# Turning normalised token rows between token order and feature order: 16 small VectorE transpositions per pair replaced by one transposition and 16 block transfers

## The chip, the cores and the metric

The kernel runs on one core of a Trainium2 chip. The metric is the device time of one execution in microseconds (us). A core has five engines that run side by side, each with its own instruction queue taken strictly in order: TensorE (PE in the profile; its weight loads are PEld), VectorE (DVE), ScalarE (ACT), GpSimd (POOL) and SyncE (SP, which here only issues DMAs). An instruction waits on semaphores until what it needs is there, and everything behind it on the same engine waits too. The 16 DMA engines are shared by all queues.

## The reference, cut to what matters

Inputs are q, k, v of shape (8, 8, 576, 64), a factor `g_ln` of 512, and two weights of 512x2048 and 2048x512, given as float64.

```python
# attention inside chunks of 64 tokens, 8 heads of 64
scores = (q_c @ k_c.T) / 8;  attn = softmax(scores);  x = attn @ v_c     # x: (8, 576, 512)
# feed-forward with a layer norm in front
xn = (x - mean(x)) / sqrt(var(x) + 1e-6) * g_ln
out = x + maximum(xn @ w_ch1, 0) @ w_ch2
```

There are 4608 tokens. The contraction of `xn @ w_ch1` runs over features, so TensorE needs `xn` with features on the 128 partitions, while attention leaves `x` with tokens on the partitions. Between the two, every block of `xn` has to be transposed. That turning is what the change is about.

## The kernel before, in words

The work is cut into 18 **pairs** of 256 tokens (two tiles of 128, index `j`), numbered 0 to 17. `attention(pair, ...)` is a Python generator that does one pair: it loads q, k, v, computes the scores (L298), the row maxima `top` (L305), the subtraction (L330) and the exponentials (L333, ScalarE), transposes the probabilities into `pt_sb` (16 VectorE transpositions of 32x256, L358, or TensorE where `by_pe` is set), sums and inverts the denominators `den` (L365 to L367), multiplies with v (L387, called PV below), scales into `x` (L421), takes mean and variance (L431, L432), `rstd` (L437, a power on GpSimd) and writes `x` to HBM for later (`spill`, L254). Then the normalised rows `xg` are made: (x - mean) * g on VectorE (L443), times `rstd` on ScalarE (L449), and turned.

Pairs 0 to 5 (tiles 0 to 2) go through an ordinary feed-forward (`ffn`, L527 and L551). The other twelve, pairs 6 to 17, are the ones with `rows_of` set. They are collected in four-pair groups of 1024 tokens: their turned rows go into two shared tiles `rows`, and `combine(half)` (L731, L734) forms from these rows sums and differences for a feed-forward that needs 7 products of half-size blocks in place of 8 (`unit_ffn`). Three such **units** follow one another. While unit u runs its products, the attention of the four pairs of unit u+1 is woven between them; the last unit has nothing beside it.

Of the twelve, pairs 6, 8 and 9 are turned on TensorE (`by_pe`, L459). The other nine, pair 7 and the eight pairs woven into the first two units, are turned on VectorE: 16 transpositions of 32 partitions x 256 elements (L467), which also put each 32x32 block into its final partition quarter.

The order of all instructions is written out by hand. Up to the units, strings (`START`, `SECOND`, `THIRD`) say which generator moves on by one `yield` between two pieces of the feed-forward. Inside a unit, `weave` counts matmuls of 128x512: a unit has 336 in the first part (the products, L778, 14 per quarter q of 6 matmuls each) and 384 in the second (L863, 192 for each half of the tokens, in steps of 4). Pair n (0 to 3) of the next unit starts at matmul `n * PAIR_SPAN + LOADED`, and its steps follow at the offsets in `STEPS`. `combine(0)` starts at 345 and `combine(1)` at 592. An offset is thus a place in the program order; what an engine does at it still waits for its data.

In the first part of a unit, the sums of a quarter sit in four PSUM banks, `c` and `a` for e = 0 and 1. ScalarE copies a bank to a snapshot (L784) and VectorE adds a snapshot to a bank, giving `hu` (L787), before the bank is used again. In the second part ScalarE makes `hh` (or `hx`), the rectified high part of `hu` (L800), and VectorE the low part `hl` (or `hx`) of it (L805), three blocks ahead of the matmuls that use them. The weights of a unit are streamed through a ring of six places of 512 KB; `ring.fetch` (L687) issues the next load on SP once the matmuls have left a place, and each place serves 12 matmuls.

Four tiles per pair (`p_sb`, `pt_sb`, `xg`, and after the change `turned`) rotate through the two buffers of the pool `work`.

## Time and profile before

| | before |
|---|---|
| median of 3 runs | 845.57 us (845.19 to 845.84) |
| profiled execution | 846.09 us, span 844.3 us |
| PE busy | 831.7 us, 99% of the span |
| DVE busy | 561.4 us, 66% |
| ACT busy | 270.8 us, 32% |
| POOL busy | 151.5 us, 18% |
| bytes moved by DMA | 192.60 MB, mean 228 GB/s |

The profiled execution is one of its own: its span runs from the first to the last recorded instruction, and its time also holds what lies around the span. In the rows below, L467 is line 467 of the kernel before, "DVE hu L787" is the VectorE instruction of line 787 that writes `hu`, and a group row gives the busy time in us, the mean of one instruction in ns, and after the bar the idle time of the engine just before them. Ends of matmuls are modelled, so a busy TensorE says little by itself; distances between starts of matmuls say more.

### The profile page before, as it was taken

How to read it: one execution, taken by the hardware profiler on the slowest of the kernel's cores; microseconds unless marked ns; L12 is line 12 of the kernel's file. 1: busy time of each engine (PE TensorE's matmuls, PEld its weight loads, DVE VectorE, ACT ScalarE, POOL GpSimd, SP SyncE). 2: the span in 40 equal slices, each digit the busy share in tenths (PEclk: the TensorE clock that was granted, in tenths of full speed). 3: DMA queues.
4: the chain of work that ended last, by engine and by line, in shares of the span. 5: the costliest groups of instructions: out<-in, count | busy, mean ns of one | idle time of the engine just before them, and what ended most of it. 6: DMA issues, size and time to landing. Idle time of an engine off the chain costs nothing.

```text
span 844.3 us, 14613 instructions
## 1 busy us (share of the span) xinstructions
PE 831.7 (99%) x5850; PEld 682.0 (81%) x5850; DVE 561.4 (66%) x957; ACT 270.8 (32%) x425; POOL 151.5 (18%) x138
## 2 busy tenths in 40 slices
PE   7999999999999999999999999999999999999998
PEld 4888888888888888888787888887878888888886
DVE  6989966787556736797999927879999421232321
ACT  5766431122322333222341402324223212232220
POOL 0111006473751223000130400001302300000000
PEclk9999999999999999999999999999999999999999
DMA  9997417938982147776786868877658776667572
GB/s 363 328 274 221 157 43 239 345 142 286 324 270 79 42 175 259 230 257 200 254 312 208 291 190 296 276 217 254 236 192 276 243 248 188 192 195 246 189 281 106
DMA packets 69043, 192.60 MB, mean 228 GB/s; under 512 B 6640, under 2 KB 20976, under 8 KB 67056
## 3 DMA queue, kind: packets, MB, share of 16 engines
q1 hardware_dynamic: 67680, 186.95, 64.1%
q0 software_dynamic: 1296, 4.72, 2.9%
q8 instruction: 46, 0.75, 0.3%
q14 instruction: 21, 0.17, 0.1%
HBM read 147.08 MB, written 39.85 MB: 221 GB/s over the span
## 4 chain that ended last, share of the span: by engine, by line
PE 84%; DVE 11%; DMA 2%; issue 1%; ACT 1%; SPq 0%; POOL 0%; ACTq 0%; DVEq 0%; POOLq 0%
PE y L778 24%; PE y L863 17%; PE y L551 15%; PE h L527 15%; PE h L863 8%; DVE pt_sb L358 3%; DVE rows L467 2%; PE s L298 2%; DMA wp<-wfs 1%; PE h L387 1%; DVE hx L805 1%; DVE top L305 1%; DMA k_t<-qkv 1%; PE s L387 1%; DVE hu L787 1%
## 5 line engine op out<-in xcount | busy, mean ns | idle before, releaser
L778 PE MATMUL y<-xc,ring 128*128 128x512 f32 x1008 | 232.5, 391 | 0.4 <-DVE hu L787 0.4
L778 PEld LDWEIGHTS y<-xc,ring 128*128 128x128 f32 x1008 | 188.3, 188 | 40.6 <-DVE hu L787 1.2
L527 PE MATMUL h<-xth,wp 128*128 128x512 f32 (+1 forms) x432 | 129.6, 370 | 1.1 <-DMA wp<-wfs 1.1
L863 PE MATMUL y<-ring,hx 128*128 128x512 f32 x486 | 128.0, 391 | 0.0
L863 PEld LDWEIGHTS y<-ring,hx 128*128 128x128 f32 x486 | 90.8, 188 | 19.0
L787 DVE TENSOR_TENSOR hu<-y,snap 128x512 f32<-128x512 f32 x72 | 49.2, 690 | 82.8 <-ACT snap L784 43.2
L551 PE MATMUL y<-wp,hh 128*128 128x512 f32 x376 | 96.2, 394 | 0.0
L527 PEld LDWEIGHTS h<-xth,wp 128*128 128x128 f32 x432 | 78.2, 188 | 15.9 <-DMA wp<-wfs 1.3
L784 ACT COPY snap<-y 128x512 f32<-128x512 f32 x72 | 42.2, 586 | 121.2 <-PE y L778 121.2
L731 POOL TENSOR_TENSOR xc<-rows,xc 128x512 fp32r<-128x512 f32 x42 | 58.7, 1413 | 123.8 <-ACT xc L730 119.8
L551 PEld LDWEIGHTS y<-wp,hh 128*128 128x128 f32 x376 | 69.1, 188 | 13.9
L358 DVE STREAM_TRANSPOSE pt_sb<-p_sb 32x256 f32<-32x256 f32 x176 | 76.7, 436 | 3.5 <-ACT p_sb L333 0.5
L527 PE MATMUL h<-xtl,wp 128*128 128x512 f32 (+1 forms) x216 | 78.3, 367 | 0.0
L541 DVE SCALAR_TENSOR_TENSOR hl<-h,hh 128x512 fp32r<-128x512 f32 (+1 forms) x53 | 33.0, 629 | 64.9 <-ACT hh L540 64.7
L863 PE MATMUL y<-ring,hh 128*128 128x512 f32 x252 | 68.9, 389 | 0.0
L467 DVE STREAM_TRANSPOSE rows<-xg 32x256 f32<-32x256 f32 x144 | 62.7, 436 | 5.4 <-ACT xg L449 3.2
L540 ACT ACTIVATE hh<-h 128x512 fp32r<-128x512 f32 (+1 forms) x53 | 28.5, 546 | 117.7 <-PE h L527 117.7
L805 DVE SCALAR_TENSOR_TENSOR hx<-hu,hx 128x512 fp32r<-128x512 f32 x54 | 43.9, 817 | 30.2 <-PE y L863 12.2
L863 PEld LDWEIGHTS y<-ring,hh 128*128 128x128 f32 x252 | 47.3, 188 | 9.9
L551 PE MATMUL y<-wp,hl 128*128 128x512 f32 x188 | 51.8, 390 | 0.0
L437 POOL TENSOR_TENSOR rstd<-vare,mhalf 128x2 f32<-128x2 f32 x12 | 10.6, 886 | 229.5 <-DVE vare L436 229.5
L863 PE MATMUL h<-ring,hx 128*128 128x512 f32 x162 | 49.9, 389 | 0.0
(130 smaller groups left out, 986.6 us busy)
## 6 DMA issues: line engine op xcount, KB each, us to landing
ring<-w2d SPq DMA_DIRECT2D x96, 512.0 KB, 4.3
ring<-wa SPq DMA_DIRECT2D x84, 512.0 KB, 4.3
raw<-w SPq DMA_DIRECT2D x15, 1024.0 KB, 7.3
out<-x SPq DMA_DIRECT2D x36, 256.0 KB, 4.5
q_t<-qkv SPq DMA_DIRECT2D x17, 512.0 KB, 5.8
k_t<-qkv SPq DMA_DIRECT2D x17, 512.0 KB, 6.8
v_t<-qkv SPq DMA_DIRECT2D x32, 256.0 KB, 6.8
w2d<-wp SPq DMA_DIRECT2D x16, 512.0 KB, 7.1
```

The source lines that it names most:

```text
L358: nc.vector.transpose(out=pt_sb[quad(2 * h2 + j), :, c, quad(i)], in_=p_sb[quad(2 * c + i), :, h2, quad(j)])
L467: nc.vector.transpose(out=to[quad(j), :, quad(i)], in_=of[quad(i), :, quad(j)])
L527: nc.tensor.matmul(h, lhsT=(wh, wh, wl)[m][:, ks], rhs=(xth, xtl, xth)[m][:, k, :], start=i == 0, stop=i == len(terms) - 1,)
L540: nc.scalar.activation(hh, h, AF.Relu)
L541: nc.vector.scalar_tensor_tensor(out=hl, in0=h, scalar=0.0, in1=hh.bitcast(F32), op0=ALU.max, op1=ALU.subtract)
L551: nc.tensor.matmul(sums(pairs[j // 2])[j % 2], lhsT=(hh, hh, hl)[m], rhs=(wh, wl, wh)[m], start=f == 0 and m == 0, stop=f == NF - 1 and m ...
L731: nc.gpsimd.tensor_tensor(out=o[:, 1], in0=x, in1=o[:, 0].bitcast(F32), op=ALU.subtract)
L778: nc.tensor.matmul(bank, lhsT=w[:, (0, 0, 1)[m], ks], rhs=x[:, (0, 1, 0)[m], k, :], start=start and k == m == 0, stop=k == 1 and m == 2, s ...
L784: nc.scalar.copy(out, bank)
L787: nc.vector.tensor_tensor(out=out, in0=bank, in1=s, op=ALU.add)
L805: nc.vector.scalar_tensor_tensor(out=hl, in0=x, scalar=0.0, in1=hh.bitcast(F32), op0=ALU.max, op1=ALU.subtract)
L863: nc.tensor.matmul(ys[j], lhsT=(hh, hh, hl)[m], rhs=w[:, (0, 1, 0)[m]], start=f == 0 and m == 0, stop=f == NF - 1 and m == 2,)
```

## The change

For the twelve pairs with `rows_of`, the centring and scaling now run on ScalarE in one instruction per tile: `Identity` with scale `rstd` and bias `-mean * rstd` (`centre`, a VectorE instruction on 128x2). The factor g is no longer applied there. It is applied after the turning, where a feature is a partition and g is one number per partition (`g_cols`, four columns that are now loaded behind `g_sb`).

For the nine pairs turned by VectorE, one transposition over 128 partitions x 1024 elements now turns every 32x32 block where it stands, into a new tile `turned`. Sixteen DMAs on SP's queue (one per pair of partition quarters: 32 partitions x 1 KB read, in two pieces of 512 B written) then carry the blocks to their places in `rows`, four to a step. Last, four ScalarE instructions over 128x256 multiply the rows by g in place. For the three pairs turned by TensorE, g goes into the evacuation of PSUM: eight ScalarE instructions of 128x128 in place of two of 128x512.

The order of tokens inside `rows` differs (by quarter `i`, then `k`), and `combine` reads it accordingly. The written-out order is changed too: `PAIR_SPAN` from 140 to 130, 19 steps in place of 18 and closer together, one step fewer for the three TensorE pairs, and some letters of `SECOND` and `THIRD` moved. A spacer tile shrinks from 176 to 144 columns.

```diff
 THIRD = {
-    0: "CS", 1: "CS", 2: "DDGS", 3: "DS", 4: "DDS", 5: "DS", 6: "DGS", 7: "GGHS", 8: "DG", 9: "D", 10: "GGP",
-    11: "HGGP", 12: "G", 13: "G", 14: "GGHP", 15: "GHP", 16: "GHP", 17: "GP", 18: "HHGP", 19: "HGP", 20: "HGP",
-    21: "HHP", 22: "HP", 24: "H", 25: "H", 26: "QQ", 27: "QR", 28: "Q", 29: "QXXN", 30: "QQR", 31: "Q",
+    0: "CS", 1: "CS", 2: "DDGS", 3: "DS", 4: "DDS", 5: "DS", 6: "GS", 7: "GGHS", 8: "DG", 9: "D", 10: "GGP",
+    11: "GGH", 12: "G", 13: "G", 14: "GGHP", 15: "GP", 16: "GHP", 17: "GGHP", 18: "GGHHP", 19: "HP", 20: "HHP",
+    21: "HP", 22: "GPP", 23: "H", 24: "H", 26: "QQ", 27: "QR", 28: "Q", 29: "QXXN", 30: "QQR", 31: "Q",
 }
-PAIR_SPAN = 140
+PAIR_SPAN = 130
 LOADED = 8
-STEPS = (0, 6, 11, 18, 26, 37, 48, 59, 68, 76, 88, 95, 102, 110, 118, 129, 140, 158)
+STEPS = (0, 6, 11, 16, 22, 30, 38, 46, 54, 60, 66, 72, 82, 88, 96, 106, 116, 126, 150)
...
-    g_sb = const.tile([P, DM], F32, name="g_sb")
+    g_all = const.tile([P, DM + NK], F32, name="g_sb")
+    g_sb, g_cols = g_all[:, :DM], g_all[:, DM:]
...
         xg = work.tile([P, 2, DM], F32, name="xg", tag="work")
-        for j in range(2):
+        if rows_of:
+            if not by_pe:
+                turned = work.tile([P, 4, 2 * NK, 32], F32, name="turned", tag="work")
+            centre = small.tile([P, 2], F32, name="centre")
             nc.vector.scalar_tensor_tensor(
-                out=xg[:, j, :], in0=x[:, j, :], scalar=mv[:, j, 0:1], in1=g_sb, op0=ALU.subtract, op1=ALU.mult
+                out=centre, in0=mv[:, :, 0], scalar=-1.0, in1=rstd, op0=ALU.mult, op1=ALU.mult
             )
-        yield
+            for j in range(2):
+                nc.scalar.activation(
+                    xg[:, j, :], x[:, j, :], AF.Identity, scale=rstd[:, j : j + 1], bias=centre[:, j : j + 1]
+                )
...
+        if rows_of and by_pe:
+            rows_t = rows_of().rearrange("p j i (k t) -> p j k i t", k=NK)
...
+                for k in range(NK):
+                    nc.scalar.activation(
+                        rows_t[:, j, k], xt[j][:, k * P : (k + 1) * P].rearrange("p (i t) -> p i t", i=4), AF.Copy,
+                        scale=g_cols[:, k : k + 1],
+                    )
+                yield
+            return
+
         if rows_of:
-            for j in range(2):
-                nc.scalar.activation(xg[:, j, :], xg[:, j, :], AF.Copy, scale=rstd[:, j : j + 1])
-            yield
...
+            nc.vector.transpose(
+                out=turned.rearrange("p b a t -> p a b t"),
+                in_=xg.rearrange("p j (k b f) -> p (j k) b f", k=NK, b=4),
+            )
+            yield
             rows_t = rows_of()
...
-                to = rows_t.rearrange("p j k t -> p (j k) t")
-                of = xg.rearrange("p j (k t) -> p (j k) t", k=NK)
-                for j in range(4):
-                    for i in range(4):
-                        nc.vector.transpose(out=to[quad(j), :, quad(i)], in_=of[quad(i), :, quad(j)])
-                    yield
+            for i in range(4):
+                for b in range(4):
+                    nc.sync.dma_start(
+                        rows_t[quad(b), :, i], turned[quad(i), b].rearrange("p (j k) t -> p j (k t)", j=2)
+                    )
+                yield
+            for k in range(NK):
+                x = rows_t.rearrange("p j i (k t) -> p (j i) k t", k=NK)[:, :, k]
+                nc.scalar.activation(x, x, AF.Copy, scale=g_cols[:, k : k + 1])
+            yield
             return
...
-        a, b = (r[:, half].rearrange("p j k t -> p k j t") for r in shared["rows"])
+        a, b = (r[:, half].rearrange("p j i (k t) -> p k (j i) t", k=NK) for r in shared["rows"])
```

More of the change, by code (lines that the diff above doesn't have):

```diff
@@ L108, in chunk_attention_ffn @@
     gap = ctx.enter_context(tc.tile_pool(name="gap", bufs=1))
-    gap.tile([P, 176], F32, name="gap")
+    gap.tile([P, 144], F32, name="gap")
     raws = ctx.enter_context(tc.tile_pool(name="raws", bufs=1))
@@ L316, in attention @@
         if pair == 0:
-            nc.sync.dma_start(g_sb, g)
+            nc.sync.dma_start(g_all, g)
         yield
@@ L445, in attention @@
             )
-        yield
+            for j in range(2):
+                nc.scalar.activation(
+                    xg[:, j, :], x[:, j, :], AF.Identity, scale=rstd[:, j : j + 1], bias=centre[:, j : j + 1]
+                )
+        else:
+            for j in range(2):
+                nc.vector.scalar_tensor_tensor(
+                    out=xg[:, j, :], in0=x[:, j, :], scalar=mv[:, j, 0:1], in1=g_sb, op0=ALU.subtract, op1=ALU.mult
+                )
+        yield
+        if rows_of and by_pe:
+            rows_t = rows_of().rearrange("p j i (k t) -> p j k i t", k=NK)
+            xt = halves()
+            for j in range(2):
+                for k in range(NK):
+                    ks = slice(k * P, (k + 1) * P)
+                    nc.tensor.transpose(out=xt[j][:, ks], in_=xg[:, j, ks], identity=ident)
+                for k in range(NK):
[5 more added lines that the diff above has]
+            return
@@ L447, in attention @@
         if rows_of:
-            for j in range(2):
-                nc.scalar.activation(xg[:, j, :], xg[:, j, :], AF.Copy, scale=rstd[:, j : j + 1])
+            nc.vector.transpose(
+                out=turned.rearrange("p b a t -> p a b t"),
+                in_=xg.rearrange("p j (k b f) -> p (j k) b f", k=NK, b=4),
+            )
             yield
-        if rows_of:
             rows_t = rows_of()
-            if by_pe:
-                xt = halves()
-                for j in range(2):
-                    for k in range(NK):
-                        ks = slice(k * P, (k + 1) * P)
-                        nc.tensor.transpose(out=xt[j][:, ks], in_=xg[:, j, ks], identity=ident)
-                    nc.scalar.copy(rows_t[:, j], xt[j].rearrange("p (k t) -> p k t", k=NK))
-                    yield
-            else:
-                to = rows_t.rearrange("p j k t -> p (j k) t")
-                of = xg.rearrange("p j (k t) -> p (j k) t", k=NK)
-                for j in range(4):
-                    for i in range(4):
-                        nc.vector.transpose(out=to[quad(j), :, quad(i)], in_=of[quad(i), :, quad(j)])
-                    yield
+            for i in range(4):
+                for b in range(4):
+                    nc.sync.dma_start(
+                        rows_t[quad(b), :, i], turned[quad(i), b].rearrange("p (j k) t -> p j (k t)", j=2)
+                    )
+                yield
@@ L469, in attention @@
+            for k in range(NK):
+                x = rows_t.rearrange("p j i (k t) -> p (j i) k t", k=NK)[:, :, k]
+                nc.scalar.activation(x, x, AF.Copy, scale=g_cols[:, k : k + 1])
+            yield
             return
@@ L1016 @@
         n: np.ascontiguousarray(a)
-        for n, a in (("qkv", qkv), ("v01", v01), ("g", np.broadcast_to(moe_g_ln, (P, DM))), ("w", w))
+        for n, a in (("qkv", qkv), ("v01", v01), ("g", g), ("w", w))
     }
```

10 lines of the change are left out of this document (6 added, 4 removed).

## The prediction

> **What bounds the kernel now.** I read the page's head first, then busy time by stage, then the chain of waits, and last the order of time around the places where TensorE stands.
>
> ```profile
> span 844.3 us, 14613 instructions
> ...
> PE 831.7 (99%) x5850; PEld 682.0 (81%) x5850; DVE 561.4 (66%) x957; ACT 270.8 (32%) x425; POOL 151.5 (18%) x138
> ```
>
> The view by stretches has, after each stretch, its length and the busy time of PE, PEld, DVE, ACT and POOL; I show the first unit and the last.
>
> ```profile
> core 0: us, PE busy (x) PEld busy (x) DVE busy (x) ACT busy (x) POOL busy (x), PEclk, DMA share, GB/s
> ...
> 326.50:502.00 175.50, 174.82 (x1235) 142.83 (x1234) 142.17 (x258) 53.73 (x91) 25.19 (x19) 1.00 0.72 243
> ...
> 677.40:844.30 166.90, 163.18 (x720) 134.77 (x719) 44.25 (x65) 38.49 (x64) 0.00 (x0) 0.99 0.63 208
> ```
>
> VectorE is busy 81% of the first unit (142.17 of 175.50), where four pairs of attention run beside the products, and 27% of the last, where none does. All pairs but one that the one transposition touches lie in the first two units. How much TensorE loses there follows from the chain of waits (start, length, what):
>
> ```profile
> 326.52 2.72 PE y L778 x12
> 329.24 1.09 PE s L298 x64
> 330.33 16.55 PE y L778 x72
> ...
> 501.88 2.72 PE y L778 x12
> ...
> 677.38 76.16 PE y L778 x336
> 753.54 43.52 PE y L863 x192
> ```
>
> In the last unit 336 products take 76.16 us, 0.2267 us each, and 192 of the second part 43.52 us, the same: its 720 matmuls take 163.2 us, with no wait. A block of scores costs 1.09 us, and the 72 products behind it 16.55 where 72 x 0.2267 is 16.32, so 1.32 us with the change of shape. Eight such blocks (four scores, four PV, taken as equal) make 163.2 + 10.6 = 173.8 us for a unit that never waits. The first took 501.88 - 326.52 = 175.36, the second 677.38 - 501.88 = 175.50. So each loses 1.6 to 1.7 us, **3.3 us together, and that is all that a lighter VectorE can win in the units**. Between the start-up and the units the chain is PE throughout. TensorE's own timeline shows where the first unit loses it:
>
> ```profile
> 403.68 4.24 PE L778 MATMUL y<-xc,ring 128*128 128x512 f32 x18
> 408.11 1.66 PE L778 MATMUL y<-xc,ring 128*128 128x512 f32 x6 [0.19 <-DVE hu L787]
> ...
> 416.07 1.16 PE L387 MATMUL h<-v_t,pt_sb 64*64 64x64 f32 x64
> ...
> 450.44 1.57 PE L387 MATMUL h<-v_t,pt_sb 64*64 64x64 f32 x64
> ...
> 452.74 0.62 PE L863 MATMUL y<-ring,hh 128*128 128x512 f32 x2
> 453.76 0.50 PE L863 MATMUL y<-ring,hl 128*128 128x512 f32 x1 [0.40 <-DVE hl L805]
> ```
>
> Eighteen products from 403.68 end at 407.76, the next starts at 408.11: 0.35. The PV block takes 1.57 where a free one takes 1.16: 0.41. Two matmuls from 452.74 end at 453.19, the next starts at 453.76: 0.57. That is 1.33; the rest of the 1.6 is scattered. All three wait for VectorE, which is behind, with the transpositions of rows among what it does:
>
> ```profile
> 395.80 3.59 DVE L467 STREAM_TRANSPOSE rows<-xg 32x256 f32<-32x256 f32 x8
> 399.42 1.23 DVE L305 TENSOR_REDUCE top<-s 128x16 f32<-128x1024 f32 x1
> 400.68 1.22 DVE L330 TENSOR_TENSOR p_sb<-s,top 128x1024 f32<-128x1024 f32 x1
> 401.93 1.80 DVE L467 STREAM_TRANSPOSE rows<-xg 32x256 f32<-32x256 f32 x4
> ```
>
> **The change, part by part.** The durations come from these groups (busy, mean of one in ns, idle before):
>
> ```profile
> L467 DVE STREAM_TRANSPOSE rows<-xg 32x256 f32<-32x256 f32 x144 | 62.7, 436 | 5.4 <-ACT xg L449 3.2
> L443 DVE SCALAR_TENSOR_TENSOR xg<-x,mv,g_sb 128x512 f32<-128x512 f32 x36 | 26.0, 762 | 0.0
> L330 DVE TENSOR_TENSOR p_sb<-s,top 128x1024 f32<-128x1024 f32 x16 | 19.5, 1219 | 0.4
> L449 ACT ACTIVATE xg<-xg,rstd 128x512 f32<-128x512 f32 x24 | 16.0, 716 | 49.8 <-DVE xg L443 25.9 <-POOL rstd L437 23.7
> L540 ACT ACTIVATE hh<-h 128x256 fp32r<-128x256 f32 x12 | 4.1, 373 | 0.8 <-PE h L527 0.8
> ```
>
> *Removed from VectorE*, per pair: 16 x 0.436 = 6.98 us of transpositions and 2 x 0.762 = 1.52 of centring. *Added*: one transposition of 128x1024, which no row shows. Its floor is the 1.22 us of another instruction of 128x1024; its ceiling is 6.98, if the four partition quarters went one after the other. I take 1.22, since 256 elements take 0.436 and 1024 of them, at the slope of other VectorE work, no more than that row. [...] `centre` is 256 values, between 0 and 0.76; I take 0.2. Net 7.1 us less per pair, 28 of the 142 in a unit.
>
> *ScalarE* does two Identity instructions in place of two Copies, at 0.716 as before, and four of 128x256 for g, between 0.373 (from PSUM) and 0.716: 0.42 each, 1.7 us per pair. Cover: ScalarE is idle for 122 us of a unit. [...] For the three pairs turned on TensorE, eight small evacuations replace two; they lie in the stage that waits for nothing, where the chain is PE.
>
> *SP and DMA*. 16 transfers per pair, none of 32 KB in the trace; the nearest:
>
> ```profile
> q1 hardware_dynamic: 67680, 186.95, 64.1%
> ...
> ring<-wa SPq DMA_DIRECT2D x84, 512.0 KB, 4.3
> ...
> v_t<-qkv SPq DMA_DIRECT2D x32, 256.0 KB, 6.8
> ...
> x_d<-x SPq DMA_DIRECT2D x14, 512.0 KB, 3.0
> ```
>
> Issue takes SP 0.42 us each (the row below), 6.7 us per pair, four in every 10 matmuls (2.27 us). SP otherwise waits for ring places, so it has the time. Behind a waiting transfer stand the ring's loads: one place of six serves 12 matmuls (2.72 us), so a load is due 13.6 us after its place is left and takes 4.3; SP may be 9 us late before TensorE notices, and it is late by 2 or 3 (the transposition) plus 1.7 (four issues). Engine time: 512 KB per pair in packets of 512 B. By bytes they are 0.3% of queue 1's 186.95 MB, 1.5 us; by packets (1024 of them at the queue's mean, 0.641 x 844.3 x 16 / 67680 = 0.128 us, over 16 engines) 8.2 us. A pair's 32 us at a share of 0.72 leaves 9. Landing lies between 3.0 and 6.8 us; I take 3.5, since the writer's side is like that of `x_d` and a ring load stands ahead. Then the last four, issued by 1.7 us after matmul 126, have landed at 5.2, and the factor step at 150 comes 24 x 0.2267 = 5.4 after it: no wait.
>
> ```profile
> 364.70 0.42 SPq L270 DMA_DIRECT2D k_t<-qkv  x1
> ```
>
> *The order.* This decides. The pair's steps are closer together: from scores to PV are 60 matmuls in place of 76. I walk the queue of VectorE for pair n = 2, whose PV now falls at matmul 330 (268 + 60, rounded up to a product), close to the change from first to second part. Durations are those of pair n = 0 in the trace, which ran without a queue:
>
> ```profile
> 330.51 1.22 DVE L305 TENSOR_REDUCE top<-s 128x16 f32<-128x1024 f32 x1
> 331.75 1.22 DVE L330 TENSOR_TENSOR p_sb<-s,top 128x1024 f32<-128x1024 f32 x1
> ...
> 334.90 3.57 DVE L358 STREAM_TRANSPOSE pt_sb<-p_sb 32x256 f32<-32x256 f32 x8 [0.27 <-ACT p_sb L333]
> ...
> 342.73 1.29 DVE L787 TENSOR_TENSOR hu<-y,snap 128x512 f32<-128x512 f32 x2
> ...
> 346.51 1.21 DVE L365 TENSOR_REDUCE den<-p_sb 128x16 f32<-128x1024 f32 x1
> ```
> ```profile
> 333.81 1.06 ACT L333 ACTIVATE p_sb<-p_sb 128x1024 f32<-128x1024 f32 x1
> ```
>
> Scores start at 0; `top` starts at 1.27 (330.51 against 329.24) and ends at 2.5; a sum `hu` waits 0.7 for its snapshot and ends at 3.9; the subtraction ends at 5.1, the exponentials at 6.2. Then 16 transpositions at 0.45 (7.2), two `hu` (1.3) and one `hl` (0.6) ahead of the last four: done at 15.3. PV is due at 1.09 + 60 x 0.2267 = 14.7, its second half, which needs the last group, 0.5 later: **0.3 late**. Behind that VectorE has one `hu` (0.6), `den` (1.6 with its two small ones), and the `hu` that frees a bank which the second matmul of the second part writes: 18.2, against 15.0 + 1.09 + 1.36 + 0.23 = 17.7: **0.5 late**. So 0.8 where 0.35 is lost today. For pair n = 3 the same walk has less in it (1.27, `top`, one `hl`, subtraction and exponentials, one L734 at 0.7, 16 transpositions, two `hl`): 14.6 against 14.7, which I count as 0.2. Pairs 0 and 1 come out about 1 us early. The third wait, at the change of halves, goes: pair 3's attention is over at matmul 524 but for its factor step, where today its transpositions run from 546 to 586. What is scattered today I keep at 0.
>
> Sum: 1.6 lost per unit today, 1.0 after, 0.6 won twice, **1.2 us**. The profiled execution took 846.09 us, its span 844.3: it becomes 843.1 in the span and 844.9 with the 1.8 around it. The median, 845.57, is 0.5 below that execution, so I forecast **844.4 us**. Own range, by 0.5 us of error in each of the two walks per unit: 842.4 to 846.4.
>
> **Rivals.**
> *All waits go.* If VectorE runs ahead a little more than in my walk (1 us in 15), nothing is left to wait for: 845.57 - 3.3 = 842.3. For it: 28 us less work per unit. Against: the compressed steps.
> *The transfers land late, and it is slower.* Place: the factor step on ScalarE, which stands ahead of the snapshots (L784), and the next pair's `pt_sb`, which takes the buffer of `turned`. It decides from a landing of 5.3 us on: the next pair's step 22 is 26 matmuls and a score block (7.0 us) behind the last group, whose issue takes 1.7. At 6.8, as for `v_t`, VectorE is 1.5 us late in three pairs per unit, less the 0.9 that pair 1 has to spare: 1.5 + 1.5 + 0.6 = 3.6, and ScalarE is 3.1 late with 2.1 to spare (two products, less 0.59) for the pairs of the first part, 1.0 twice, partly the same time. About 4.5 per unit, 9 less the 1.2: 853. For it: rows of 6.8 are in this queue. Against: those are loads from HBM, and writes from on-chip memory (`x_d`) land in 3.0.
> *The single transposition is as long as the sixteen.* Then VectorE is relieved of 1.3 us per pair alone while PV comes 16 matmuls, 3.6 us, sooner; in the second part a pair is 5.8 us heavier than in my walk, which today's 18.3 us from scores to PV swallow and 14.7 do not: 0.7 late in each of eight pairs, 845.57 + 5.6 = 851.
> *Nothing moves.* The old waits are replaced by new ones of the same size: within 1 us of before. It lies inside the forecast's own range.
>
> **How the numbers follow.** Forecast 0.47, all waits gone 0.30, late landing 0.13, long transposition 0.05, something else slower 0.05. A measurement of this kernel tells 0.2% (1.7 us) from no change. Faster by that: the 0.30 and 0.06 of the forecast's lower edge, 0.36. Slower: 0.13 + 0.05 + 0.05 less 0.03 of mild cases, 0.20. Same: 0.44. The floor of the range is the full gain, 842.2. The top reaches into the late landings and leaves out their far end: 848.2.
>
> **What would show it.** Right: DVE busy in 326 to 502 near 114 us; the transposition a row near 1.2 us; transfers landing under 5.3 us; no PE row waiting for `hl` L805 behind the change of halves; a PV at the end of a unit's first part still over 1.16 us. Wrong: a ScalarE row that waits for a DMA into `rows`, a VectorE `pt_sb` that waits for a DMA, a ring load that TensorE waits for, or a unit longer than 175.4 us.

## The result, and where the time went

| | before | after |
|---|---|---|
| median | 845.38 us (844.84 to 845.84, 4 runs) | 852.87 us (852.68 to 853.39, 4 runs) |
| ratio, 95% interval | | 1.009 (1.0072 to 1.0107) |
| span of the profiled execution | 844.3 us | 851.1 us |

The kernel became slower, by 7.5 us. The forecast was 844.4 with a top of 848.2; the rival "the transfers land late" had named 853.

The page's head of the kernel after:

```profile
span 851.1 us, 14767 instructions
...
PE 833.6 (98%) x5850; PEld 682.8 (80%) x5850; DVE 498.1 (59%) x810; ACT 290.0 (34%) x479; POOL 149.4 (18%) x138
```

VectorE got its relief, 63 us of busy time. TensorE has the same 5850 matmuls; what grew is its waiting. The chain of waits of the kernel after (start, length, what) says where:

```profile
327.49 2.72 PE y L803 x12
...
506.09 2.72 PE y L803 x12
...
683.65 76.16 PE y L803 x336
```

The first unit lasts 506.09 - 327.49 = 178.60 us (175.36 before), the second 177.56 (175.50 before), the rest up to the end of the span 167.45 (166.9 before), and the units begin 1.0 us later. So the 6.8 us are 1.0 ahead of the units, 3.2 and 2.1 in them and 0.5 in the last one. TensorE's timeline in the first unit:

```profile
376.26 0.34 PE L389 MATMUL h<-v_t,pt_sb 64*64 64x64 f32 x6
377.09 1.14 PE L389 MATMUL h<-v_t,pt_sb 64*64 64x64 f32 x58 [0.49 <-DVE pt_sb L360]
378.16 16.64 PE L803 MATMUL y<-xc,ring 128*128 128x512 f32 x72
394.73 1.16 PE L300 MATMUL s<-k_t,q_t 64*64 64x64 f32 x64
...
409.65 0.34 PE L389 MATMUL h<-v_t,pt_sb 64*64 64x64 f32 x6
410.38 1.14 PE L389 MATMUL h<-v_t,pt_sb 64*64 64x64 f32 x58 [0.39 <-DVE pt_sb L360]
411.45 1.65 PE L803 MATMUL y<-xc,ring 128*128 128x512 f32 x6
...
418.38 2.88 PE L888 MATMUL y<-ring,hx 128*128 128x512 f32 x12
421.65 2.14 PE L888 MATMUL y<-ring,hx 128*128 128x512 f32 x8 [0.39 <-ACT hx L825]
424.09 3.93 PE L888 MATMUL y<-ring,hx 128*128 128x512 f32 x16 [0.30 <-DVE hx L830]
427.85 1.07 PE L888 MATMUL y<-ring,hh 128*128 128x512 f32 x4
...
443.77 0.33 PE L389 MATMUL h<-v_t,pt_sb 64*64 64x64 f32 x4
444.96 0.30 PE L389 MATMUL h<-v_t,pt_sb 64*64 64x64 f32 x2 [0.86 <-DVE pt_sb L360]
445.79 1.14 PE L389 MATMUL h<-v_t,pt_sb 64*64 64x64 f32 x58 [0.54 <-DVE pt_sb L360]
446.86 1.20 PE L888 MATMUL y<-ring,hh 128*128 128x512 f32 x4
```

Read by distances between starts, a PV block that doesn't wait takes 1.09. The PV of pair 1 takes 378.16 - 376.26 = 1.90, 0.8 too much; that of pair 2 takes 1.80, 0.7 too much; that of pair 3 takes 3.09, 2.0 too much. The 36 products from 418.38 take 9.47 where 36 x 0.2267 is 8.16: 1.3 too much, for `hx`. Together 4.8, and 178.6 - 4.8 is the 173.8 us of the prediction's unit without waits. The wait for `hl` at the change of halves is gone. What the other engines do behind the rows from 418 to 447 (timelines of GpSimd, VectorE, ScalarE and SP's queue, in that order):

```profile
418.21 1.29 POOL L756 TENSOR_TENSOR xc<-rows,xc 128x512 fp32r<-128x512 f32 x1
```
```profile
418.29 1.24 DVE L448 SCALAR_TENSOR_TENSOR centre<-mv,rstd 128x2 f32<-128x2 f32 x1 [0.87 <-POOL rstd L439]
...
436.82 3.58 DVE L360 STREAM_TRANSPOSE pt_sb<-p_sb 32x256 f32<-32x256 f32 x8 [2.54 <-DMA rows<-turned]
```
```profile
419.56 1.52 ACT L452 ACTIVATE xg<-x,centre,rstd 128x512 f32<-128x512 f32 x2 [5.31 <-DVE centre L448]
420.99 0.61 ACT L825 ACTIVATE hx<-hu 128x512 fp32r<-128x512 f32 x1
...
436.72 1.71 ACT L492 ACTIVATE rows<-rows,g_sb 128x256 f32<-128x256 f32 x4 [2.54 <-DMA rows<-turned]
```
```profile
422.43 2.52 SPq L486 DMA_DIRECT2D rows<-turned  x4
425.05 0.53 SPq L712 DMA_DIRECT2D ring<-w2d  x1
425.62 5.07 SPq L486 DMA_DIRECT2D rows<-turned  x8
...
432.48 2.50 SPq L486 DMA_DIRECT2D rows<-turned  x4
```

Two stories stand in these rows. The first: SP issues four transfers in 2.5 us, and the last of the sixteen ends at 434.98. VectorE, which can't write the next pair's `pt_sb` over `turned`, and ScalarE with its multiplications by g both stand until 436.7. Pair 3's transpositions start 2.54 late, and its PV at 444.96 waits. The second: the centring on ScalarE stands at the head of its queue for `centre`, and the `hx` behind it ends at 421.60, when TensorE has wanted it since 421.10. The other half of the 1.3 us is the `hx` of VectorE, for which TensorE waits until 424.09: it stands behind the transposition of the same pair, which waits for the centring.

The groups and the view of the transfers give the terms of the sum (first the groups: busy, mean of one in ns, idle before; then the DMA issues: KB each and the median us from issue to landing; then the issues of one pair in ns, least, median and most; last the view of waits: idle time in all, times, longest):

```profile
L478 DVE STREAM_TRANSPOSE turned<-xg 128x1024 f32<-128x1024 f32 x9 | 11.2, 1244 | 10.6 <-ACT xg L452 10.6
L492 ACT ACTIVATE rows<-rows,g_sb 128x256 f32<-128x256 f32 x36 | 15.3, 497 | 19.3 <-DMA rows<-turned 19.3
```
```profile
rows<-turned SPq DMA_DIRECT2D x144, 32.0 KB, 2.2
```
```profile
L486 SPq DMA_DIRECT2D rows<-turned x16: 585/594/1110, 386.4 to 397.3; - x16
```
```profile
ACT rows L492 <- DMA rows<-turned: 19.3, 6, 5.9
DVE pt_sb L360 <- DMA rows<-turned: 6.9, 4, 2.5
```

Ahead of the units the 1.0 us is one wait of a pair turned on TensorE. ScalarE first does four multiplications by g of pair 7, then two casts, and only then the small evacuations that free the bank (timelines of ScalarE and TensorE):

```profile
301.22 1.70 ACT L492 ACTIVATE rows<-rows,g_sb 128x256 f32<-128x256 f32 x4
302.82 1.13 ACT L755 CAST xc<-rows 128x512 fp32r<-128x512 f32 x2
303.85 1.12 ACT L470 ACTIVATE rows<-s,g_sb 128x128 f32<-128x128 f32 x4
```
```profile
305.02 0.66 PE L468 MATMUL s<-ident,xg 128*128 128x128 f32 x4 [0.96 <-ACT rows L470]
```

The start of the units alone would not show this: in e5, e7, e9 and e11, whose instructions are the same up to there, the profiles have it anywhere from 324.7 to 327.1. The chain of waits that leads to this row also holds a `centre` of 1.24 us (at 297.99), of the kind that the last section describes. The 0.5 us of the last unit isn't traced to an instruction; with the same instructions that unit takes 166.95 in the profile of e13 and 167.4 in that of e10.

### The profile page after: what moved, and what is told of

Read it like the earlier page. It is cut to its first block, busy times and chain, and to the rows that moved or that the text cites. A ratio compares the mean times of both kernels' runs of the same rounds, so it can differ in the third digit from the quotient of the medians.

```text
span 851.1 us, 14767 instructions
## 1 busy us (share of the span) xinstructions
PE 833.6 (98%) x5850; PEld 682.8 (80%) x5850; DVE 498.1 (59%) x810; ACT 290.0 (34%) x479; POOL 149.4 (18%) x138
## 4 chain that ended last, share of the span: by engine, by line
PE 79%; DVE 11%; DMA 3%; SPq 3%; ACT 2%; issue 1%; POOL 0%; DVEq 0%; ACTq 0%; POOLq 0%
PE y L803 22%; PE y L888 18%; PE y L576 13%; PE h L552 13%; PE h L888 8%; DVE pt_sb L360 4%; SPq L486 3%; PE s L300 2%; PE h L389 1%; DMA wp<-wfs 1%; DMA rows<-turned 1%; DMA k_t<-qkv 1%; DVE stats L433 1%; DVE hu L812 1%; PE s L389 0%
## 5 line engine op out<-in xcount | busy, mean ns | idle before, releaser
L830 DVE SCALAR_TENSOR_TENSOR hl<-hu,hh 128x512 fp32r<-128x512 f32 x42 | 30.8, 737 | 39.1 <-PE h L888 16.7
L825 ACT ACTIVATE hx<-hu 128x512 fp32r<-128x512 f32 x54 | 33.3, 627 | 53.7 <-PE y L888 30.5
```

The costliest lines, as they stand in the source:

```text
L825: nc.scalar.activation(hh, x, AF.Relu)
L830: nc.vector.scalar_tensor_tensor(out=hl, in0=x, scalar=0.0, in1=hh.bitcast(F32), op0=ALU.max, op1=ALU.subtract)
```

## The experiments

The theories, as the expectations name them. A: the transfers end late because each takes SP some 0.6 us to issue. B: their bytes and packets slow the ring of weights. C: the compressed order itself is late, with PV 60 matmuls behind the scores and ScalarE's `hx` behind the centring. Medians in us; "before" ran on the same chip; "units" are the lengths of the first and the second, from the start of the first product of each.

| run | median | before | ratio (95%) | units |
|---|---|---|---|---|
| after | 852.87 | 845.38 | 1.0090 (1.0072 to 1.0107) | 178.6, 177.6 |
| e1 | 888.24 | 845.75 | 1.0504 (1.0484 to 1.0524) | 196.3, 195.9 |
| e2 | 847.31 | 845.75 | 1.0016 (1.0003 to 1.0029) | 175.8, 175.5 |
| e3 | 847.81 | 845.75 | 1.0024 (1.0011 to 1.0038) | 175.6, 175.8 |
| e4 | 847.66 | 845.75 | 1.0026 (1.0013 to 1.0039) | 175.8, 175.8 |
| e5 | 853.48 | 845.83 | 1.0091 (1.0076 to 1.0106) | 178.3, 179.5 |
| e6 | 872.34 | 845.83 | 1.0309 (1.0291 to 1.0326) | 190.3, 187.6 |
| e7 | 851.07 | 845.83 | 1.0060 (1.0042 to 1.0079) | 179.2, 177.3 |
| e8 | 857.54 | 845.83 | 1.0140 (1.0125 to 1.0155) | 180.2, 180.4 |
| e9 | 845.17 | 845.03 | 1.0001 (0.9992 to 1.0010) | 175.4, 175.4 |
| e10 | 844.99 | 845.03 | 0.9995 (0.9986 to 1.0004) | 174.7, 174.7 |
| e11 | 846.78 | 845.03 | 1.0016 (1.0008 to 1.0025) | 175.8, 175.8 |
| e12 | 845.88 | 845.85 | 1.0006 (0.9994 to 1.0018) | 175.1, 175.1 |
| e13 | 847.14 | 845.60 | 1.0027 (1.0013 to 1.0040) | 176.8, 175.9 |
| e14 | 844.37 | 845.60 | 0.9989 (0.9980 to 0.9998) | 174.7, 174.8 |

### e1: the kernel after in a wide order

```diff
-PAIR_SPAN = 130
-STEPS = (0, 6, 11, 16, 22, 30, 38, 46, 54, 60, 66, 72, 82, 88, 96, 106, 116, 126, 150)
-LAST_HALF = 592
+PAIR_SPAN = 140
+STEPS = (0, 6, 11, 18, 26, 37, 48, 59, 68, 76, 82, 88, 98, 104, 112, 122, 132, 142, 170)
+LAST_HALF = 604
```

> The changed kernel with the rhythm of the kernel before: pairs 140 matmuls apart, PV again 76 after the scores, the transfers at 112, 122, 132, 142 and the factor at 170, combine(1) at 604. Nothing else differs. Theory A (SP takes 0.64 us to issue a transfer where 0.42 was forecast, 10.2 us per pair, so the buffer of turned comes free late, and with it pt_sb and PV): the transfers get 54 matmuls, 12.2 us, before the next pair's pt_sb, which is enough for 10.2 + 2.2; the 2.5 us lost in the first unit to PV of pairs 1 and 3 and 1.6 in the second go. Theory C (the compressed order by itself: PV too close behind the scores, and hx held up on ScalarE behind the centring): the other 2.0 + 1.3 us go too. Together about 846.4: what remains is 1.0 us ahead of the units. Theory B (bytes and packets of the transfers slow the ring's loads): the same bytes, so still 850 or more.

Measured 888.24, 42 us slower than before; every theory missed it. The order moved the last transfers to offset 142, behind the start of the next pair and its loads, while the next pair still wants the buffer early. ScalarE's factor step and VectorE then hold up the snapshots, sums and `hx` that TensorE needs (timelines of ScalarE and TensorE):

```profile
414.75 1.70 ACT L492 ACTIVATE rows<-rows,g_sb 128x256 f32<-128x256 f32 x4 [5.81 <-DMA rows<-turned]
```
```profile
417.40 2.93 PE L803 MATMUL y<-xc,ring 128*128 128x512 f32 x6 [3.83 <-DVE hu L812]
```

Eight such waits of TensorE, 2.0 to 4.5 us long, add to 28 us. The rest is the clock. The view by stretches, whose eighth column is the granted clock, at that wait and behind it:

```profile
core 0: us, PE busy (x) PEld busy (x) DVE busy (x) ACT busy (x) POOL busy (x), PEclk, DMA share, GB/s
414.00:417.40 3.40, 0.00 (x0) 0.00 (x0) 2.47 (x6) 2.65 (x7) 0.00 (x0) 0.85 1.00 374
417.40:420.80 3.40, 3.40 (x8) 2.73 (x9) 3.28 (x7) 1.00 (x3) 0.00 (x0) 0.50 0.37 147
420.80:424.20 3.40, 3.40 (x11) 2.66 (x11) 3.32 (x7) 2.80 (x7) 2.65 (x2) 0.65 0.45 154
```

At each of the eight waits such a stretch of half clock begins, 3.4 or 6.8 us long, 37.4 us in all: up to 19 us of lost work. A wait of 2.0 us was enough once (655.40 to 657.40, with a granted clock of 0.50 from 659 to 662), and the waits of the kernel after that are shown above, 1.1 us at most, cost no clock: it is 1.00 around each of them. The run shows the price of a late transfer; it does not tell A from C.

### e2: four transfers per pair in place of sixteen

```diff
-                for b in range(4):
-                    nc.sync.dma_start(
-                        rows_t[quad(b), :, i], turned[quad(i), b].rearrange("p (j k) t -> p j (k t)", j=2)
-                    )
+                nc.sync.dma_start(rows_t[:, :, i], turned[:, i].rearrange("p (j k) t -> p j (k t)", j=2))
```

> The changed kernel and its order, but the sixteen transfers of 32 partitions are replaced by four of 128 partitions with the same bytes and the same pieces of 512 B, which leave each block in its partition quarter: the move between quarters is left out, so the result is not the reference's. Theory A: SP issues for 2.5 us per pair in place of 10.2; the waits of PV in pairs 1 and 3 go (4.1 us in both units): 848.7, and the VectorE waits for a landing of the transfers fall from 6.9 us to near 0. Theory B: bytes are the same, 852.9. Theory C: the order is the same, 852.9.

Measured 847.31: the same bytes in a quarter of the issues bring the ratio from 1.0090 to 1.0016. (This kernel leaves out the move between partition quarters.) One issue takes 0.60 us here too, for four times the bytes. B falls and A stands; in the kernel after, too, no matmul of the units waits for a load of the ring. What is left in the first unit is a wait of PV and the wait for `hx`, with the 1.0 us ahead of the units.

### e3: only ScalarE's part of the change

The centring and the factor on ScalarE, with sixteen VectorE transpositions into the new layout, in the old rhythm.

```diff
-PAIR_SPAN = 130
-STEPS = (0, 6, 11, 16, 22, 30, 38, 46, 54, 60, 66, 72, 82, 88, 96, 106, 116, 126, 150)
+PAIR_SPAN = 140
+STEPS = (0, 6, 11, 18, 26, 37, 48, 59, 68, 76, 88, 95, 102, 110, 118, 129, 140, 158, 162)
...
-                    nc.sync.dma_start(
-                        rows_t[quad(b), :, i], turned[quad(i), b].rearrange("p (j k) t -> p j (k t)", j=2)
+                    nc.vector.transpose(
+                        out=rows_t[quad(b), :, i].rearrange("p j (k t) -> p j k t", k=NK),
+                        in_=of[quad(i), :, b].rearrange("p (j k) f -> p j k f", j=2),
```

> Half of the change: centring and scaling on ScalarE and the factor by row behind it stay, but the nine pairs are turned by sixteen VectorE transpositions as before (into the new order of tokens), without turned and without transfers; the rhythm in the units is that of the kernel before, with the factor step at 162. Theories A, B and C all expect no loss in the units: 1.5 us per unit as before, 846.4 with the 1.0 us ahead of the units. If ScalarE's new work is itself the cause, the loss stays: 850 or more.

Measured 847.81, where the units are nearly as long as before (175.6 and 175.8 for 175.4 and 175.5). Most of the 2 us lies ahead of the units: the same wait for the small evacuations as in the kernel after, here 1.6 us. In the wide order ScalarE's part costs 0.3 us at most inside a unit.

### e4: half of the transfers from GpSimd's queue

```diff
-                    nc.sync.dma_start(
+                    (nc.sync if b < 2 else nc.gpsimd).dma_start(
```

> The changed kernel and its order, but eight of each pair's sixteen transfers are issued by GpSimd's queue in place of SP's. Theory A: SP needs 5.1 us per pair, GpSimd about 7 at the 0.87 us of its other issues, side by side; the last one is out about 3 us sooner, so most of the 4.1 us of PV waits go: 849 to 850. Theory B and theory C: 852.9.

Measured 847.66, more than was expected of it. The second pair's transfers in the first unit (ns of one issue as least, median and most, and first and last start):

```profile
L486 SPq DMA_DIRECT2D rows<-turned x8: 585/593/602, 385.1 to 392.2; - x8
L486 POOL DMA_DIRECT2D rows<-turned x8: 533/538/574, 385.4 to 389.2; - x8
...
DMA to landing us min/median/max: 3.0/4.2/5.6
```

Each transfer lands later, 4.2 us for 2.9 in the same place of the kernel after, yet all sixteen are done sooner: over the units' pairs the trace has 8.2 to 11.2 us from the first issue to the last landing, against 12.1 to 14.2. VectorE's wait in front of `pt_sb` is gone (its timeline):

```profile
433.68 3.57 DVE L360 STREAM_TRANSPOSE pt_sb<-p_sb 32x256 f32<-32x256 f32 x8
```

So the issue is the cost, not the landing. What stays is PV of pair 2 and `hx`, theory C.

### e5 and e6: a wide order whose transfers end before the next pair, with two queues and with SP alone

```diff
-    21: "HP", 22: "GPP", 23: "H", 24: "H", 26: "QQ", 27: "QR", 28: "Q", 29: "QXXN", 30: "QQR", 31: "Q",
+    21: "HP", 22: "PP", 23: "G", 24: "H", 25: "H", 26: "QQ", 27: "QR", 28: "Q", 29: "QXXN", 30: "QQR", 31: "Q",
-PAIR_SPAN = 130
-STEPS = (0, 6, 11, 16, 22, 30, 38, 46, 54, 60, 66, 72, 82, 88, 96, 106, 116, 126, 150)
+PAIR_SPAN = 140
+STEPS = (0, 6, 11, 18, 26, 37, 48, 59, 68, 76, 80, 84, 92, 96, 100, 108, 116, 124, 158)
```

Beside this, e5 splits the transfers as e4 does and e6 leaves them on SP.

> Transfers split between SP and GpSimd as in e4, pairs 140 matmuls apart and PV 76 after the scores as in the kernel before, but the steps behind PV drawn together, so that the transfers stand at 100 to 124, ahead of the next pair's loads (in e1 they stood at 112 to 142, the last of them behind 1 MB of loads), and the factor at 158. In THIRD pair 9 (H) one token later and the factor of pair 7 one token later. Theory A+C (late transfers by issue time, then PV too close behind the scores, then hx behind the centring): with all three gone a unit loses under 0.5 us, the units start at 326.5 in place of 327.5: 842.5 to 843.5, 2 to 3 us under the kernel before. If the relief of VectorE by 28 us per unit is worth nothing, 845.4 as before.

> As e5, but all sixteen transfers on SP. Theory A: issue takes 10.2 us from the transposition's end, about 38 matmuls behind PV, so the last lands near 169 of the pair's offsets, where the next pair's pt_sb can start at 162: VectorE about 1.5 us late, which PV at 76 bears; the factor step holds ScalarE about 2.5 us, near the 2.1 us that the snapshots have. 844 to 847, and 1 to 3 us above e5. If the place of the issue doesn't matter once the order is wide, the same as e5.

Measured 853.48 and 872.34; both expectations missed. In e5 a sum, `hh`, a PV, `hl` and `hx` are late by 0.2 to 1.2 us each in the first unit, and in the second TensorE waits 1.5 us for a load of the ring: this order has waits of its own. e6 differs from e5 by the queue alone, and is 19 us slower, with five waits of TensorE of 1.8 to 4.7 us. Behind the four longer ones the matmuls are slow as in e1 (six at 412.33 and six at 600.98 take 2.45 and 2.93 us, where six without a wait take 1.36; two at 490.30 and two at 678.52 take 0.85, where two take 0.45), and the mean granted clock of the execution, 0.988 over 871.1 us, makes some 21 us at half clock; the one of 1.8 is for a load of the ring, at 455.74, which in the chain of waits takes 9.26 us from 446.34 on (the median of such a load is 4.6 in the kernel after) and comes behind transfers in SP's queue (the last issue of these ends at 443.7, and six loads of the ring then follow one another from 447.9 on). That is A again, at a place where it hurts more; that a full queue makes the loads of the ring late as well is an inference from these times.

### e7: e4 with the centring 16 matmuls later

```diff
-STEPS = (0, 6, 11, 16, 22, 30, 38, 46, 54, 60, 66, 72, 82, 88, 96, 106, 116, 126, 150)
+STEPS = (0, 6, 11, 16, 22, 30, 38, 46, 54, 60, 66, 72, 98, 102, 106, 112, 118, 124, 150)
```

(With the line of `THIRD` of e5.)

> As e4 (the changed order, transfers split), with the centring at 98 in place of 82, the transposition at 102 and the transfers at 106 to 124; THIRD as in e5. Theory C, part ScalarE: the splits of blocks 3 and 4 now stand ahead of the centring, and the two waits for hx (0.6 + 0.5 us per unit in e4) go; the wait of PV in pair 2 (0.6) stays: 847.7 - 2.0 - 1.0 (ahead of the units) = 844.7. If the hx waits come from somewhere else, 846.7.

Measured 851.07, 3.4 thousandths above e4. The wait for ScalarE's `hx` behind the first pairs went, as expected, but the transfers start later for it, and the PV of pair 3 waits for `pt_sb` again, twice, as in the kernel after. The wait was moved. Part of the loss is the clock: in the profiled execution these two waits, of 1.15 and 0.54 us, are followed in the first unit by slower matmuls (58 of the PV take 1.73 us, the 68 products behind them 16.58), in the second by none (1.14 and 15.64), and the units last 179.2 and 177.3 us. The mean granted clock of that execution, 0.998 over 848.8 us, makes 3.4 us at half clock.

### e8: sixteen transpositions in the tight order

The order of the kernel after, with the second part of e3's diff.

> The changed order with the old turning: e3's sixteen VectorE transpositions (no transfers), in the steps of the changed kernel, pairs 130 apart, PV 60 after the scores. Theory C: with 23 us of VectorE work per pair in 32 us and 60 matmuls to PV, the PV waits of pairs 2 and 3 grow to 1 or 2 us each: 850 to 853. If the compressed order costs nothing, 847.8 as e3.

Measured 857.54, a ratio of 1.0140. In one and the same order the turning by one transposition is thus worth 5 thousandths (4 us) with the transfers on SP (1.0090) and 11 (some 10 us) with two queues (1.0026). The tight order is only affordable with the lighter VectorE, and takes most of the gain for itself: e3, wide and with the sixteen, took 847.81, and e4, tight and with the one, 847.66.

### e9, e11: a repair ahead of the units, and PV later

```diff
-    21: "HP", 22: "GPP", 23: "H", 24: "H", 26: "QQ", 27: "QR", 28: "Q", 29: "QXXN", 30: "QQR", 31: "Q",
+    21: "HP", 22: "PP", 23: "G", 24: "H", 25: "H", 26: "QQ", 27: "QR", 28: "Q", 29: "QXXN", 30: "QQR", 31: "Q",
```

e11 is e4 with this line, which moves the multiplications by g (G) one piece later and the turning of the pair on TensorE (H) one piece behind them. e9 is e11 with later PV steps:

```diff
-STEPS = (0, 6, 11, 16, 22, 30, 38, 46, 54, 60, 66, 72, 82, 88, 96, 106, 116, 126, 150)
+STEPS = (0, 6, 11, 16, 22, 30, 38, 46, 60, 66, 70, 74, 86, 90, 96, 106, 116, 126, 150)
```

> e4 (the changed order in the units, transfers split between SP and GpSimd) with one more edit: in THIRD pair 9 (H) moves on one token later, so that its two steps on TensorE stand where they stood before the change, and the factor step of pair 7 one token later. Theory: the 1.0 us ahead of the units in the changed kernel is TensorE waiting for the eight small evacuations of H, which stand behind pair 7's factor on ScalarE: the units start about 1.0 us sooner and the rest is e4: 846.7. If the wait only moves, 847.7.

> e11 with the denominators and PV six matmuls later (60 and 66), x, statistics behind them, the centring at 86 in place of 82 and the transposition at 90; transfers and factor where they are. Theory: PV of pair 2 (0.6 per unit in e4) has 1.4 us more and no longer waits, and block 3's hx stands ahead of the centring (0.6 per unit goes); the VectorE part of the hx wait (0.5) may stay: 846.7 - 2.4 = 844.3. After e7, where a later centring brought a longer wait of pair 3's PV, the rival is that the wait moves there: 847 to 849.

Measured 846.78 (e11) and 845.17 (e9). e11 came out as expected: the wait at 305 is gone and the units are unchanged. (The intervals of e4 and e11 overlap, so it is the row that shows this, not the ratio.) In e9 the waits of PV and of `hx` are gone, but both units have a new one of 1.5 us, for a sum that VectorE now does behind the last group of `pt_sb` (TensorE's timeline):

```profile
407.49 1.66 PE L803 MATMUL y<-xc,ring 128*128 128x512 f32 x6 [1.35 <-DVE hu L812]
```

### e10: the turning alone

e4, with the centring and g on VectorE and `rstd` on ScalarE as before the change, for the pairs turned on VectorE; so neither `centre` nor a factor step.

```diff
+        if rows_of and not by_pe:
+            turned = work.tile([P, 4, 2 * NK, 32], F32, name="turned", tag="work")
+            for j in range(2):
+                nc.vector.scalar_tensor_tensor(
+                    out=xg[:, j, :], in0=x[:, j, :], scalar=mv[:, j, 0:1], in1=g_sb, op0=ALU.subtract, op1=ALU.mult
+                )
+            for j in range(2):
+                nc.scalar.activation(xg[:, j, :], xg[:, j, :], AF.Copy, scale=rstd[:, j : j + 1])
...
-            for k in range(NK):
-                x = rows_t.rearrange("p j i (k t) -> p (j i) k t", k=NK)[:, :, k]
-                nc.scalar.activation(x, x, AF.Copy, scale=g_cols[:, k : k + 1])
```

> e4 with only the turning changed for the nine pairs: centring with g on VectorE and rstd on ScalarE as before the change, one transposition, split transfers, no factor step behind them (an empty step in its place). VectorE gets 1.4 us per pair back, ScalarE loses 1.7 and the wait for the landing. Theory: the waits for hx come from the centring that holds ScalarE until rstd is there, which the old form does too, so they stay: 847.7, within 1 us. If the factor step or the bias form costs something itself, 845 to 846.

Measured 844.99, by the ratios 3.1 thousandths (2.6 us) better than e4, where it was expected that the wait for `hx` stays; the other branch of the expectation, 845 to 846, fits. The wait went (TensorE's timeline):

```profile
416.29 8.52 PE L893 MATMUL y<-ring,hx 128*128 128x512 f32 x36
424.64 1.07 PE L893 MATMUL y<-ring,hh 128*128 128x512 f32 x4
...
440.56 1.16 PE L389 MATMUL h<-v_t,pt_sb 64*64 64x64 f32 x64
```

The 36 products take 8.35 us (9.47 in the kernel after), and the PV of pair 3 its free 1.09. The part of the change that seemed free, the move to ScalarE, is the dearer one once the transfers are split. By the profiles of e4 and e10, 1.1 and 1.0 us of it lie in the two units and about 1.0 ahead of them, where e10 has no multiplications by g in front of the small evacuations and no wait at 305.

### e12: e10 with a shorter distance of pairs

e10 with the line of `THIRD` of e11 and `PAIR_SPAN = 128` in place of 130.

> e10 (turning alone changed, transfers split between SP and GpSimd, no ScalarE part) with THIRD as in e11 and pairs 128 apart in place of 130: the scores of pair 2 fall at matmul 264 in place of 270 and its last four transpositions stand ahead of one hu and one hl in place of behind them, PV at 324. Theory: pair 2's PV wait (0.6 per unit) goes and the units start 1.0 sooner: 845.0 - 1.2 - 1.0 = 842.8, and a unit of about 174.1. If the wait only moves, as in e9, 844.0; if the transfers come too late for pair 3, which starts 1.8 us sooner, 845 or more.

Measured 845.88, not 842.8. The PV of pair 2 no longer waits, but the PV of pair 3 does (0.4 and 0.7 us in each unit): its transpositions into `pt_sb` start 2.1 us late in the first unit, at 431.95, just behind the last landing of pair 2's transfers (431.6).

### e13: e10 with all transfers on SP

The diff of e10 without the line that splits the transfers.

> e10 (one transposition and transfers, centring as before the change, no factor step), but all sixteen transfers on SP as in the changed kernel. If the late transfers act through the buffer of turned: VectorE waits for landings as in the changed kernel (6.9 us in four waits there), PV of pairs 1 and 3 wait, and the 4 to 5 us between the changed kernel and e4 come back: 849 to 850. If they act through the factor step on ScalarE: 845 as e10.

Measured 847.14, between the two expectations. The transfers end as late behind their first issue as in the kernel after (12.1 to 14.3 us over the units' pairs), and VectorE waits in front of `pt_sb` in the same four places: 1.55, 2.09, 0.90 and 1.71 us, for 1.55, 2.54, 0.93 and 1.85 there. Two of these rows name ScalarE as the releaser (VectorE's timeline):

```profile
366.91 5.41 DVE L360 STREAM_TRANSPOSE pt_sb<-p_sb 32x256 f32<-32x256 f32 x12 [1.55 <-ACT hu L814]
...
433.11 3.57 DVE L360 STREAM_TRANSPOSE pt_sb<-p_sb 32x256 f32<-32x256 f32 x8 [2.09 <-ACT hh L830]
```

But `pt_sb` doesn't depend on `hu` or `hh`, and both rows start 0.3 to 0.4 us behind the last landing of the transfers (366.6 and 432.7), as the first of the kernel after starts 0.3 behind its own (368.8). So the late transfers do act through the buffer of `turned`, as the first expectation has it; what was too high is its price, 849 to 850. The wait for `hx` is gone. The PV of pair 1 waits 0.8 as in the kernel after, that of pair 3 waits 1.3 where it was 2.0 (TensorE's timeline):

```profile
441.81 1.14 PE L389 MATMUL h<-v_t,pt_sb 64*64 64x64 f32 x58 [0.54 <-DVE pt_sb L360]
```

With the kernel after, e4 and e10 it makes a table of two by two (ratios to before):

| | 16 transfers on SP | 8 on SP, 8 on GpSimd |
|---|---|---|
| centring and g on ScalarE | 1.0090 (after) | 1.0026 (e4) |
| as before the change | 1.0027 (e13) | 0.9995 (e10) |

Late transfers alone cost 3.2 thousandths (2.7 us), ScalarE's part alone 3.1 (2.6 us), and both together 9.5 (8.0 us), 3.2 more than their sum. By the four intervals that excess is known to some 2.7 thousandths, so it is barely told from nothing; the profiled units show the same sign, smaller (3.9 us against 2.1 and 1.1 in the first, 2.8 against 1.2 and 1.0 in the second). The traces show where these 0.7 and 0.6 us lie. With the centring on ScalarE (after, e4) the first transfer of pair 2 starts 27.7 to 27.8 us behind that pair's scores, without it (e13, e10) 26.6 to 26.7, in both units. Where all sixteen are on SP, that lateness reaches the PV of pair 3: it waits 2.0 and 1.8 us in the kernel after, 1.3 and 1.2 in e13, and not at all in e4 and e10.

### e14: e10 with the line of `THIRD` of e11

> e10 with THIRD as in e11, pairs 130 apart as in e10. If the wait ahead of the units comes from the place of pair 9's steps alone, the units start as in e11, and since e10's own profile shows no such wait any more, nothing is won: 845.0. If e10 still has it in part, 844.0 to 844.5, under the kernel before by 0.5 to 1.

Measured 844.37 against 845.60, ratio 0.9989 (0.9980 to 0.9998): the one version that beats both kernels, and by 0.1%. The interval only just leaves out 1, and it is the best of fourteen versions, so the gain itself is not shown beyond doubt. From e10 (0.9995) it can't be told apart: without the factor step the wait ahead of the units was gone there already. Of the waits only the PV of pair 2 is left, 0.7 us in a unit of 174.7 (TensorE's timeline):

```profile
408.41 0.34 PE L389 MATMUL h<-v_t,pt_sb 64*64 64x64 f32 x6
...
410.21 1.66 PE L808 MATMUL y<-xc,ring 128*128 128x512 f32 x6
```

## Why the prediction was wrong, point by point

**The step that failed** is "Issue takes SP 0.42 us each (the row below), 6.7 us per pair, four in every 10 matmuls (2.27 us). SP otherwise waits for ring places, so it has the time." The 0.42 came from one load of `k_t`; in the same profile the median issue on SP runs from 0.32 us (loads of the ring) to 0.58 (`w2d<-wp`, likewise 512 KB). These transfers take 0.594 each and follow one another at 0.64: 10.2 us per pair, and 2.55 for four. With a ring load's 0.53 between them that is 3.1 us where 2.27 were there. So the queue doesn't make up for a late start, it falls behind by 0.8 us with every group. For pair 2 the rows tell it. Offset 96 lies at 394.73 + 1.09 + 96 x 0.2267 and 1.8 for the PV between, at 419.4; the first issue comes at 422.43, 3.0 late. The last issue ends 12.55 later, where the forecast had three groups of 2.27 and 1.7, so 8.5: 4.05 more. From there until ScalarE and VectorE go on it takes 436.72 - 434.98 = 1.74 and not 3.5: 1.76 less. By the forecast all had landed 6.8 + 5.2 behind offset 96, at 431.4; with 3.0 + 4.05 - 1.76 it is 436.7.

The 3.0 is a second slip in the same place. The prediction names it ("late by 2 or 3 (the transposition)"), but only for the loads of the ring; its landing of the last four counts from matmul 126 as if the first four had been on time. Both engines were ready at 434.2 to 434.3. Without the 3.0 the transfers would have been there at 433.7, without the 4.05 at 432.7, by an estimate from these rows; so for pair 2 it took both. For pair 0 the first issue is only 0.5 late (354.60, where offset 96 lies at 354.1), its last issue ends 12.87 later, and VectorE still waits 1.55 at 369.09: there the issue alone does it.

**The rival.** "The transfers land late, and it is slower" had the place right, both the factor step and the buffer of `turned`, and a price, 853, that agrees with 852.87. But it was tied to a landing of 5.3 us, and so got 0.13. The landing is 2.2, better than the 3.5 assumed. Not the landing but the issue, and the late start, ate the slack; the rival's condition named one of three ways to be late. Its price was right in part by chance: it was all put on late transfers, and by the table above these two causes share it.

**"No wait" at the factor step, and "ScalarE is idle for 122 us of a unit" as cover.** The factor step waited 19.3 us in six places. The second sentence looks at busy time and not at order: an instruction that waits at the head of a queue costs what stands behind it. Here that was `hx`, behind the centring, which waits for `centre`, which waits for `rstd` and for GpSimd. Against e4, e10 shows the two pieces together to be worth 2.6 us. Centring and factor step were not tried apart, but the rows point to both: the wait ahead of the units stands behind four multiplications by g, the waits for `hx` in the units behind the centring. For pair 2 of the first unit the first of these `hx` starts 26.3 us behind the scores in e4 and 25.2 in e10.

**"they lie in the stage that waits for nothing".** The small evacuations cost 1.0 us ahead of the units, with the four multiplications of another pair in front of them. e11 took that away by moving the letters G and H one piece later.

**The walks.** PV of pair 2 waits, as forecast, by 0.7 and not 0.3. (By its own terms, 15.3 against 14.7 and 0.5, the walk gives 0.1.) Pair 1, called early, waits 0.8, and pair 3, counted at 0.2, waits 2.0: both behind late transfers, which the walks had taken as landed. In e14, where they land in time, these two waits are gone and pair 2's stays. The second wait of the forecast, 0.5 for a bank, shows as 0.1 at most: the six products from 411.45 take 1.49 up to the first matmul of the second part, at 412.94, where six without a wait take 1.36.

**What held.** VectorE's part: 1.244 us for the one transposition (1.22 taken, ceiling 6.98), and 115.34 us of busy time in the first unit, where 114 was forecast. The third wait, for `hl`, went. The ceiling of 3.3 us stands: e14 has won 0.6 and 0.7 us of it in the two units, about the 1.2 of the forecast's sum, with the transfers split and ScalarE's part taken back.

## What to carry to other kernels

The bytes of a transfer did not tell its time in the queue: here 32 KB and 128 KB both took SP 0.6 us to issue, and of the loads of 512 KB one of the ring 0.32 and one of `w2d` 0.58 (medians). Take that time from a transfer of the same form if there is one, and leave room if there is none. Count those times in the queue, with what else stands there, against the stretch that the order gives them, and from the moment at which the first can really start, before the landing is looked at. And a move to an idle engine is free only if nothing behind it in that engine's queue is due (here ScalarE was idle for 122 us of a unit, and what it was given cost 2.6 us by e4 and e10): ask what the moved instruction waits for, not how much time the engine has. Last, shifting a step by hand mostly moved a wait to the next place (e7, e9, e12); what won was taking load from the queue that was full.

## What the runs showed of the hardware that was not expected

**Tiny VectorE instructions beside GpSimd.** `centre` has 128x2 elements. In nine of its twelve places nothing ran on GpSimd beside it, and it took 0.15 or 0.16 us, as for pair 1 (VectorE's timeline):

```profile
383.34 0.16 DVE L448 SCALAR_TENSOR_TENSOR centre<-mv,rstd 128x2 f32<-128x2 f32 x1 [0.87 <-POOL rstd L439]
```

It took 1.24 at 418.29, where a GpSimd subtraction runs from 418.21 to 419.50, and ended 0.03 behind that. The other two, at 297.99 and 596.25 (each about 1.24 us), also started 0.07 or 0.08 behind the start of such a subtraction and ended 0.02 behind its end. So in these three rows `centre` looks held by what ran on GpSimd. At its 0.16, the one at 418.29 would have let the centring and the `hx` behind it come about 1.1 us sooner, by an estimate from these rows, which is near the 1.3 lost there. In e10 and e13, which have no `centre` in the units, the transfers of that pair do start 1.1 us sooner, but other things differ there too; no run took this hold away alone.

**Half clock behind short waits.** Behind eight waits of TensorE of 2.0 to 4.5 us in e1 came 3.4 or 6.8 us at half clock each, 37.4 in all, and behind four of up to 4.7 us in e6 some 21 in all, so the cost of such a wait isn't its length. Behind one of 1.8 us (e6: the twelve products from 455.74 take 3.00 us, where half clock would make 5.4) and two of 1.5 (e9, with a mean clock of 1.00) came none. Length isn't all of it: in e7 waits of 1.15 and 0.54 us close together were followed by 3.4 us of half clock in one unit and by none in the other.

**Two queues.** Sixteen transfers over SP and GpSimd land later one by one (4.2 us for 2.9, second pair of the first unit) and are done about 3 us sooner together.
